# Grouped-query attention, start and sharing of the exponentials: K of group 1 by a transposed load, third chunk by bank, VectorE's exponentials in chunks 3, 9, ... 381

## Chip, cores and metric

The kernel runs on one core of one Trainium2 chip. The metric is the device time of one execution in microseconds (us). All runs are fast ones, at a granted clock of 0.996 or more of the full one.

## The reference

```python
B, Hq, Hkv, Sq, Sk, D = 16, 32, 8, 288, 512, 128      # bf16
k = jnp.repeat(k, rep, axis=1); v = jnp.repeat(v, rep, axis=1)   # rep = 4
scores = jnp.einsum("bhqd,bhkd->bhqk", q, k) * D ** -0.5
out = jnp.einsum("bhqk,bhkd->bhqd", softmax(scores, axis=-1), v)
```

There are 128 groups (16 x 8), each with 1152 queries that share 512 keys and values.

## The kernel before

The scores of a group, transposed, are 4608 columns of 128 partitions, cut into three chunks of 1536 columns (three banks of PSUM, the memory that TensorE writes to; a bank holds 512 of these columns). So there are 384 chunks, 0 to 383. For chunk n TensorE makes the scores (`op_s`), ScalarE takes the exponential, and two chunks later TensorE multiplies P by V (`op_pv`); VectorE divides by the row sums and evicts (`op_rc`, `op_ev`). In every sixth chunk VectorE takes the last 120 columns of the exponential itself, by a polynomial in eight operations.

```python
# TensorE: one chunk of scores, then P times V two chunks behind
for n in range(NS):
    op_s(n)
    if shared(n): op_sy(n)                 # 120 columns into the spare end of a bank of ps_o
    if n == 2: op_kt(1, range(NJ), 1)      # transposes of K, group 1
    if n >= LAG: op_pv(n - LAG)
...
# VectorE, for r in range(NS - 1), n = r + 2
op_rc(r)
if shared(n): op_y(n)
if shared(n - 1): op_yu(n - 1, 1); op_yu(n - 1, 2); op_yp(n - 1)
op_ev(r)
if shared(n): op_yb(n); op_ym(n); op_yu(n, 0)
...
# GpSimd: V of group g from the landing buffer into a padded one
waits = [have("v", g)]
if g >= 2: waits.append(("s_pv", NC * (g - 2) + 2))
emit(eng, waits, lambda: eng.tensor_copy(v_sb[...], vd_sb[...]))
...
# SyncE issues every transfer but two, in a fixed order
first = [q(0), v(0), q(1), k(2..3), v(1..3), q(2), q(3)]       # (shortened)
```

P times V of the first and second chunk of a group also reads part of the next chunk (`place`, `sequence`).

Of the kernel before, what the change touches and what calls it, by code (L numbers as in the profile page):

```python
# [9 lines left out]
BF16 = mybir.dt.bfloat16  # L10
# [121 lines left out]
def bass_standalone__gqa_softmax__near_ridge_kernel(  # L132
# [6 lines left out]
    B, Hq, Sq, D = q.shape  # L139
    _, Hkv, Sk, _ = k.shape  # L140
    P = 128
    R = (Hq // Hkv) * Sq
    NJ = Sk // P
# [8 lines left out]
    NC = COLS // CH  # L152
# [10 lines left out]
    EVERY = 6  # L163
# [3 lines left out]
    UG = 4  # L167
# [2 lines left out]
    NQ = 12  # L170
    NPT = 6
    WARM = 5
    FIRST = 2
    FIRST_SHARED = 6
    AHEAD = 1.08
    NO = 12
    NS = NG * NC
# [5 lines left out]
    k_v = k.rearrange("b g (p j) d -> (b g p) (j d)", j=NJ)  # L183
    kd_v = k.rearrange("b g (p j) d -> p (b g) (j d)", j=NJ)
# [3 lines left out]
    with ExitStack() as es:  # L188
        sem = {}
# [13 lines left out]
            S("us_v%d" % i)  # L203
        for i in range(UG):
            S("s_k%d" % i)
        for name in ["s_v0", "s_v1", "s_s0", "s_y", "s_yb", "s_ym", "s_yu", "s_yp", "s_kd0", "s_kd1", "s_id", "s_kp"]:
            S(name)
        for i in range(NQ):
            S("s_q%d" % i)
# [25 lines left out]
        main = ExitStack()  # L235
        vd_sb = main.enter_context(nc.sbuf_tensor("vd_sb", [P, NSLOT, UG, NJ * D], BF16))
        v_sb = main.enter_context(nc.sbuf_tensor("v_sb", [P, NSLOT, UG * NJ, VP], BF16))
        qt_sb = main.enter_context(nc.sbuf_tensor("qt_sb", [P, NQ, NT, P], BF16))
        kd_sb = main.enter_context(nc.sbuf_tensor("kd_sb", [P, 2, NJ * D], BF16))
        ident = main.enter_context(nc.sbuf_tensor("ident", [P, P], BF16))  # L240
        ones_b = main.enter_context(nc.sbuf_tensor("ones_b", [P, P], BF16))
        kt_sb = main.enter_context(nc.sbuf_tensor("kt_sb", [P, NSLOT, NJ, UG, P], BF16))
# [18 lines left out]
        def need(eng, waits):  # L261

            left = []
            for (s, n) in waits:
                key = (id(eng), s)
                if seen.get(key, 0) < n:
                    seen[key] = n
                    left.append((sem[s], n))
            return left

        def emit(eng, waits, fn):
            waits = need(eng, waits)
            for (s, n) in waits[:-1]:
                eng.wait_ge(s, n)
            ins = fn()
            if waits:
                ins.wait_op(waits[-1][0], waits[-1][1], "sem-ge")
            return ins



        def op_kd(eng, g):
            eng.dma_start(kd_sb[:, g], kd_v[:, g]).then_inc(sem["s_kd%d" % g], 16)

        def op_k(u, g0=0):
            eng = nc.sync
            sl = u % NSLOT
            if u >= NSLOT:
                for (s, n) in need(eng, [("s_s", NC * UG * (u - NSLOT + 1))]):
                    eng.wait_ge(s, n)  # L290
            eng.dma_start_transpose(
                kt_sb[:, sl, :, g0:UG].rearrange("d j g p -> d j (g p)"),
                k_v[(u * UG + g0) * P:(u + 1) * UG * P]
            ).then_inc(sem["us_k%d" % sl if u > 0 else "s_k2"], 16)

        def op_v(u, eng=None, g0=0, g1=UG):
            eng = eng or nc.sync
            sl = u % NSLOT
            if u >= NSLOT:
                for (s, n) in need(eng, [("s_vc", UG * (u - NSLOT + 1))]):  # L300
                    eng.wait_ge(s, n)
            eng.dma_start(
                vd_sb[:, sl, g0:g1], v_v[:, u * UG + g0:u * UG + g1]
            ).then_inc(sem["us_v%d" % sl if u > 0 else "s_v%d" % g0], 16)

        def op_q(g):
            eng = nc.sync
            if g >= NQ:
                for (s, n) in need(eng, [("s_s", NC * (g - NQ + 1))]):
                    eng.wait_ge(s, n)  # L310
            eng.dma_start_transpose(qt_sb[:, g % NQ], q_v[g * P:(g + 1) * P]).then_inc(sem["s_q%d" % (g % NQ)], 16)
# [11 lines left out]
        def have(kind, g):  # L323

            u = g // UG
            if u == 0 and kind == "k":
                return ("s_k%d" % min(g, 2), (2, 1, 16)[min(g, 2)])
            if u == 0:
                return ("s_v%d" % min(g, 1), 16)
            return ("us_%s%d" % (kind, u % NSLOT), 16 * (u // NSLOT + (0 if u % NSLOT == 0 else 1)))  # L330
# [43 lines left out]
        def ready(n, x):  # L374

            if n < FIRST and x < TPC - 1:
                return ("s_eb", n * (TPC - 1) + x + 1)
# [18 lines left out]
            i, c = place(t, j)  # L396
            return pt_sb[:, (g * NC + i) % NPT, c:c + P]

        def op_kt(g, tiles, bank):

            eng = nc.tensor
            dst = ps_o[:, bank].bitcast(BF16)
            for x, j in enumerate(tiles):
                ins = emit(eng, [("s_id", 2), ("s_kd%d" % g, 16)], lambda: eng.transpose(  # L404
                    dst[:, x * P:(x + 1) * P], kd_sb[:, g, j * D:(j + 1) * D], ident[:]))
            ins.then_inc(sem["s_kp"], 1)

        def op_kc(g, tiles, bank, n):
            eng = nc.vector
            src = ps_o[:, bank].bitcast(BF16)[:, 0:len(tiles) * P].rearrange("d (j p) -> d j p", p=P)  # L410
            emit(eng, [("s_kp", n)], lambda: eng.tensor_copy(  # L411
                kt_sb[:, 0, tiles[0]:tiles[-1] + 1, g], src)).then_inc(sem["s_k%d" % g], 1)

        def op_warm(n, w, dst):

# [101 lines left out]


        def shared(n):
            return FIRST_SHARED <= n < NS - NC and (n - FIRST_SHARED) % EVERY == 0  # L520

        def nth(n):
            return (n - FIRST_SHARED) // EVERY + 1
# [100 lines left out]


        first = [lambda: op_q0(0), lambda: op_v(0, None, 0, 1)]
        first += [lambda: op_q(1), lambda: op_k(0, 2), lambda: op_v(0, None, 1, UG), lambda: op_q(2), lambda: op_q(3)]

        sp = []
        for u in range(1, NU):  # L630
# [21 lines left out]
        @block.tensor  # L652
        def _(eng):
            op_warm(WARM, BANK, ps_o[:, 1])
            op_warm(1, P, ps_o[:, 1])
            op_kt(0, range(1), 0)
            op_kt(0, range(1, NJ), 1)
            op_warm(1, P, ps_s[:, 1])
            for n in range(NS):
                op_s(n)  # L660
                if shared(n):
                    op_sy(n)
                if n == 2:
                    op_kt(1, range(NJ), 1)
                if n >= LAG:
                    op_pv(n - LAG)
            op_pv(NS - 2)
            op_pv_last()
            emit(eng, [("s_ev", NS - 2), ("s_bad", 2)], lambda: eng.matmul(  # L669
                ps_o[0:1, NS % 2, 0:ALONE + 1], one_f[:], bad_sb[:, 1, :], start=True, stop=True)  # L670
            ).then_inc(sem["s_bad"], 1)
            choose(eng, "pe")

        @block.scalar
        def _(eng):
            op_kd(eng, 0)
            eng.activation(dum[:], nc.const_aps.tensor(0.0, [P, 1], FP32), ACTF.Exp)
            for (s, n) in need(eng, [("s_k0", 2)]):
                eng.wait_ge(s, n)
            op_kd(eng, 1)  # L680
            for n in range(NS):
                op_exp(n)
            op_ev_act()
            choose(eng, "act")
# [12 lines left out]
        @block.vector  # L697
        def _(eng):
            eng.memset(one_f[:], 1.0)
            op_kc(0, range(1), 0, 1)  # L700
            op_kc(0, range(1, NJ), 1, 2)
            op_kc(1, range(NJ), 1, 3)
            per_b = G * NC
            w0 = NS - 1 - ALONE // TPC
            last = rl_sb[:, NG * NT - ALONE:NG * NT]
            for r in range(NS - 1):
                n = r + LAG
                op_rc(r)
                if shared(n):
                    op_y(n)  # L710
                if shared(n - 1):
                    op_yu(n - 1, 1)
                    op_yu(n - 1, 2)
                    op_yp(n - 1)
                op_ev(r)
                if shared(n):
                    op_yb(n)
                    op_ym(n)
                    op_yu(n, 0)
                if r % per_b == per_b - 1 and r < NS - 1:  # L720
                    op_stat(r // per_b)
                if r == w0:
                    op_stat(B - 1)
                if r == w0 + 1:
                    emit(eng, [("s_stat", B)], lambda: eng.tensor_reduce(
                        ck_sb[:, 0:1], st_sb[:, 0, :], AX.X, ALU.max))
                    eng.tensor_reduce(ck_sb[:, 1:2], st_sb[:, 1, :], AX.X, ALU.min).then_inc(sem["s_stat"], 1)
                if r == w0 + 2:
                    op_over(ck_sb[:, 0:1], ck_sb[:, 1:2], ALONE, ALONE + 1, ("s_stat", B + 1), B + 2)
            op_rc(NS - 1)  # L730
            op_ev_last()
            op_over(last, last, 0, ALONE, ("s_rc", NS), B + 3)
            with nc.allow_low_precision(reason="a count of at most 2048"):
                emit(eng, [("s_bad", 3)], lambda: eng.tensor_reduce(  # L734
                    flag_i[:], ps_o[0:1, NS % 2, 0:ALONE + 1], AX.X, ALU.add)).then_inc(sem["s_flag"], 1)
            choose(eng, "dve")
# [30 lines left out]
```

## Time and profile before

| | before |
|---|---|
| median of three runs | 521.98 us (521.74 to 523.07) |
| span of the profiled run | 519.98 us |
| chunk 7 starts on ScalarE | 14.61 us |
| last chunk starts | 514.87 us |
| from chunk 7 to the last | 500.26 us, 376 chunks, 1.3305 each |
| from the start of the last exponential (third bank, 515.82) to the end | 4.16 us |

The last four rows cut the span into a start, a middle and an end. The prediction shows the lines of the page.

### The profile page before, as it was taken

What the parts mean: (1) busy time and instruction counts of PE and PEld (TensorE: products, weight loads), DVE (VectorE), ACT (ScalarE), POOL (GpSimd) and SP (SyncE); (2) the same over time, 40 slices, a digit from 0 to 9 for tenths busy, and PEclk for the clock granted to TensorE, in tenths of its full rate; (3) what the DMA queues carried; (4) which work ended last, traced back from release to release, by engine and by line L of the source; (5) the groups of instructions that cost most, each with busy time, mean ns of one, the idle gap of its engine ahead of it and who ended that gap; (6) DMA issues with size and microseconds to landing.
All of it is one profiled execution on the core that took longest, in us unless ns stands there. A gap on an engine that the chain in (4) does not pass through costs nothing.

```text
span 520.0 us, 15243 instructions
## 1 busy us (share of the span) xinstructions
PE 510.3 (98%) x6118; PEld 394.6 (76%) x6224; DVE 369.6 (71%) x1315; ACT 513.3 (99%) x393; POOL 79.8 (15%) x135
## 2 busy tenths in 40 slices
PE   8999999999999999999999999999999999999997
PEld 5777777777777777777777777777777777777776
DVE  2767767777777677676776776767767767677776
ACT  7999999999999999999999999999999999999997
POOL 2111111111111111111111111111111111111110
PEclk9999999999999999999999999999999999999999
DMA  9999999999999998999999989999998989998212
GB/s 186 237 218 230 267 194 248 225 213 210 219 233 256 208 245 201 235 248 240 215 241 209 209 225 220 241 185 209 229 240 232 227 194 201 192 234 198 86 69 93
DMA packets 253078, 110.06 MB, mean 212 GB/s; under 512 B 219728, under 2 KB 236752, under 8 KB 253008
## 3 DMA queue, kind: packets, MB, share of 16 engines
q1 hardware_dynamic: 252720, 108.82, 97.7%
q8 instruction: 49, 0.80, 0.7%
q10 hardware_dynamic: 288, 0.26, 0.2%
q14 instruction: 21, 0.17, 0.2%
HBM read 17.04 MB, written 37.75 MB: 105 GB/s over the span
## 4 chain that ended last, share of the span: by engine, by line
ACT 98%; DMA 1%; issue 1%; DVE 0%; PE 0%
ACT pt_sb L516 97%; DMA qt_sb<-in_q_dram 1%; ACT pt_sb L511 1%; PE ps_s L439 0%; DVE o_sb L585 0%; DVE o_sb L595 0%; PE ps_s L479 0%; DVE rl_sb L575 0%; PE ps_o L669 0%; DVE bad_sb L621 0%; DVE flag_i L734 0%; DVE bad_sb L618 0%
## 5 line engine op out<-in xcount | busy, mean ns | idle before, releaser
L516 ACT ACTIVATE pt_sb<-ps_s 128x1536 bf16<-128x1536 f32 (+2 forms) x384 | 508.8, 1441 | 0.0
L479 PE MATMUL ps_o<-v_sb,pt_sb 128*128 128x129 bf16 x4584 | 322.3, 220 | 1.1
L479 PEld LDWEIGHTS ps_o<-v_sb,pt_sb 128*128 128x128 bf16 x4584 | 282.8, 98 | 49.7 <-DVE o_sb L585 14.1
L439 PE MATMUL ps_s<-qt_sb,kt_sb 128*128 128x512 bf16 (+2 forms) x1430 | 290.4, 320 | 5.0 <-DMA qt_sb<-in_q_dram 0.5
L585 DVE TENSOR_TENSOR o_sb<-ps_o,rl_sb 128x384 bf16<-128x384 f32 x382 | 211.9, 555 | 9.3 <-DVE rl_sb L575 0.5
L439 PEld LDWEIGHTS ps_s<-qt_sb,kt_sb 128*128 128x128 bf16 x1536 | 123.9, 98 | 62.3 <-issue 1.1
L575 DVE RECIPROCAL rl_sb<-ps_o 128x3 f32<-128x3 f32 x382 | 68.1, 178 | 125.5 <-PE ps_o L479 124.0
L568 POOL COPY v_sb<-vd_sb 128x512 bf16<-128x512 bf16 x128 | 78.8, 616 | 429.1 <-PE ps_o L479 408.9
L549 DVE SCALAR_TENSOR_TENSOR u_sb<-u_sb,m_sb 128x120 f32<-128x120 f32 x126 | 35.6, 283 | 2.2
L556 DVE SCALAR_TENSOR_TENSOR pt_sb<-u_sb,e_sb 128x120 bf16<-128x120 f32 x63 | 17.8, 283 | 2.2
L549 DVE SCALAR_TENSOR_TENSOR u_sb<-m_sb 128x120 f32<-128x120 f32 x63 | 17.4, 277 | 0.0
L527 DVE TENSOR_SCALAR y_sb<-ps_o 128x120 f32<-128x120 f32 x63 | 15.9, 253 | 0.0
L540 DVE TENSOR_SCALAR m_sb<-t_sb 128x120 int32<-128x120 int32 x63 | 14.1, 223 | 2.2
L540 DVE TENSOR_SCALAR e_sb<-t_sb 128x120 int32<-128x120 int32 x63 | 13.6, 216 | 0.0
L450 PE MATMUL ps_o<-qt_sb,kt_sb 128*128 128x120 bf16 x63 | 13.6, 216 | 0.0
L533 DVE TENSOR_SCALAR t_sb<-y_sb 128x120 int32<-128x120 f32 x63 | 13.4, 213 | 0.0
L450 PEld LDWEIGHTS ps_o<-qt_sb,kt_sb 128*128 128x128 bf16 x63 | 6.2, 98 | 7.4
L511 ACT ACTIVATE pt_sb<-ps_s 128x512 bf16<-128x512 f32 x6 | 3.3, 616 | 2.3 <-PE ps_s L439 2.3
L411 DVE COPY kt_sb<-ps_o 128x128 bf16<-128x128 bf16 (+2 forms) x3 | 1.0, 336 | 6.2 <-PE ps_o L404 6.1
L613 DVE TENSOR_REDUCE st_sb<-rl_sb 128x1 f32<-128x72 f32 (+1 forms) x16 | 3.5, 216 | 0.0
L611 DVE TENSOR_REDUCE st_sb<-rl_sb 128x1 f32<-128x72 f32 (+1 forms) x16 | 3.5, 216 | 0.0
L417 PE MATMUL ps_o<-const-bfloat16-1.0 128*128 128x512 bf16 (+1 forms) x6 | 2.4, 570 | 0.9 <-PEq L752 0.9
(32 smaller groups left out, 12.0 us busy)
## 6 DMA issues: line engine op xcount, KB each, us to landing
out_dram<-o_sb SPq DMA_DIRECT2D x127, 288.0 KB, 3.7
vd_sb<-in_v_dram SPq DMA_DIRECT2D x31, 512.0 KB, 5.5
qt_sb<-in_q_dram SPq DMA_TRANSPOSE x128, 4.9
kt_sb<-in_k_dram SPq DMA_TRANSPOSE x32, 5.1
vd_sb<-in_v_dram SPq DMA_DIRECT2D x1, 384.0 KB, 4.6
out_dram<-o_sb SPq DMA_DIRECT2D x3, 96.0 KB, 1.6
kd_sb<-in_k_dram ACTq DMA_DIRECT2D x2, 128.0 KB, 2.7
vd_sb<-in_v_dram SPq DMA_DIRECT2D x1, 128.0 KB, 3.3
```

Source lines behind the costliest of these rows:

```text
L439: ins = emit(eng, w_x, lambda: eng.matmul(ps_s[:, n % 2, c:c + w], kt_sb[:, sl, j, gi, :], qg[:, t * P:t * P + w], start=True, stop=True))
L450: emit(eng, [("s_ev", n - LAG - 1)], lambda: eng.matmul(ps_o[:, (n - LAG) % 2, BANK - W:BANK], kt_sb[:, (g // UG) % NSLOT, j, g % UG, :], ...
L479: ins = emit(eng, w_x, lambda: eng.matmul(outs(r)[:, t - r % NC * TPC, :], pt(g, t, j), v_sb[:, sl, gi * NJ + j, 0:DV], start=(x == 0), st ...
L516: emit(eng, waits, lambda: eng.activation(d, s, ACTF.Exp, scale=scale)).then_inc(sem["s_e"], 1)
L527: emit(eng, [("s_yb", nth(n) - NB), ("s_pv", n - LAG + 1)], lambda: eng.tensor_scalar(out=y_sb[:, b], in0=ps_o[:, (n - LAG) % 2, BANK - W: ...
L533: emit(eng, [("s_ym", 2 * (nth(n) - NB)), ("s_y", nth(n))], lambda: eng.tensor_scalar(out=t_sb[:, b], in0=y_sb[:, b], scalar1=Y_MUL, scala ...
L540: emit(eng, [("s_yp", nth(n) - NB), ("s_yb", nth(n))], lambda: eng.tensor_scalar(out=dst[:, b], in0=t_sb[:, b], scalar1=mask, scalar2=bits ...
L549: lambda: eng.scalar_tensor_tensor(out=u_sb[:, b, x], in0=src, scalar=QUARTIC[x], in1=m, op0=ALU.add, op1=ALU.mult)
L556: lambda: eng.scalar_tensor_tensor(out=pt_sb[:, n % NPT, CH - W:CH], in0=u_sb[:, b, 2], scalar=QUARTIC[3], in1=e_sb[:, b].bitcast(FP32), o ...
L568: emit(eng, waits, lambda: eng.tensor_copy(v_sb[:, sl, gi * NJ:(gi + 1) * NJ, 0:D], vd_sb[:, sl, gi].rearrange("p (j d) -> p j d", d=D))). ...
L575: emit(eng, [("s_pv", r + 1)], lambda: eng.reciprocal(rl_sb[:, TPC * r:TPC * (r + 1)].unsqueeze(2), outs(r)[:, :, D:DV])).then_inc(sem["s_ ...
L585: emit(eng, waits, lambda: eng.tensor_tensor(out=o_sb[:, g % NO, t0:t0 + TPC, :], in0=outs(r)[:, :, 0:D], in1=rl_sb[:, TPC * r:TPC * (r + ...
```

## The change

Its intent: K of group 1 no longer takes TensorE and VectorE but arrives transposed; the third chunk is exponentiated bank by bank so that what reads it can begin earlier; VectorE helps three chunks sooner and once more at the end.

```diff
-    FIRST = 2
-    FIRST_SHARED = 6
+    FIRST = 3
+    FIRST_SHARED = 3
...
-            return FIRST_SHARED <= n < NS - NC and (n - FIRST_SHARED) % EVERY == 0
+            return FIRST_SHARED <= n < NS - 2 and (n - FIRST_SHARED) % EVERY == 0
...
-        first += [op_q(1), op_k(0, 2), op_v(0, None, 1, UG), op_q(2), op_q(3)]              # "lambda:" left out
+        first += [op_q(1), op_k(0, 1, 2), op_v(0, None, 1, UG), op_k(0, 2), op_q(2), op_q(3)]
...
-                if n == 2:
-                    op_kt(1, range(NJ), 1)
...
-            for (s, n) in need(eng, [("s_k0", 2)]):
-                eng.wait_ge(s, n)
-            op_kd(eng, 1)
...
-            op_kc(1, range(NJ), 1, 3)
```

(The rest of the diff fits the helpers to one direct load of K.)

More of the change, by code (lines that the diff above doesn't have):

```diff
@@ L205, in bass_standalone__gqa_softmax__near_ridge_kernel @@
             S("s_k%d" % i)
-        for name in ["s_v0", "s_v1", "s_s0", "s_y", "s_yb", "s_ym", "s_yu", "s_yp", "s_kd0", "s_kd1", "s_id", "s_kp"]:
+        for name in ["s_v0", "s_v1", "s_s0", "s_y", "s_yb", "s_ym", "s_yu", "s_yp", "s_kd0", "s_id", "s_kp"]:
             S(name)
@@ L238, in bass_standalone__gqa_softmax__near_ridge_kernel @@
         qt_sb = main.enter_context(nc.sbuf_tensor("qt_sb", [P, NQ, NT, P], BF16))
-        kd_sb = main.enter_context(nc.sbuf_tensor("kd_sb", [P, 2, NJ * D], BF16))
+        kd_sb = main.enter_context(nc.sbuf_tensor("kd_sb", [P, NJ * D], BF16))
         ident = main.enter_context(nc.sbuf_tensor("ident", [P, P], BF16))
@@ L278, in emit, with op_kd, op_k @@
             return ins
-        def op_kd(eng, g):
-            eng.dma_start(kd_sb[:, g], kd_v[:, g]).then_inc(sem["s_kd%d" % g], 16)
-        def op_k(u, g0=0):
+        def op_kd(eng):
+            eng.dma_start(kd_sb[:], kd_v[:, 0]).then_inc(sem["s_kd0"], 16)
+        def op_k(u, g0=0, g1=UG):
             eng = nc.sync
@@ L291, in op_k @@
             eng.dma_start_transpose(
-                kt_sb[:, sl, :, g0:UG].rearrange("d j g p -> d j (g p)"),
-                k_v[(u * UG + g0) * P:(u + 1) * UG * P]
-            ).then_inc(sem["us_k%d" % sl if u > 0 else "s_k2"], 16)
+                kt_sb[:, sl, :, g0:g1].rearrange("d j g p -> d j (g p)"),
+                k_v[(u * UG + g0) * P:(u * UG + g1) * P]
+            ).then_inc(sem["us_k%d" % sl if u > 0 else "s_k%d" % g0], 16)
         def op_v(u, eng=None, g0=0, g1=UG):
@@ L326, in have @@
             if u == 0 and kind == "k":
-                return ("s_k%d" % min(g, 2), (2, 1, 16)[min(g, 2)])
+                return ("s_k%d" % min(g, 2), (2, 16, 16)[min(g, 2)])
             if u == 0:
@@ L397, in pt, with op_kt @@
             return pt_sb[:, (g * NC + i) % NPT, c:c + P]
-        def op_kt(g, tiles, bank):
+        def op_kt(tiles, bank):
             eng = nc.tensor
@@ L403, in op_kt, with op_kc @@
             for x, j in enumerate(tiles):
-                ins = emit(eng, [("s_id", 2), ("s_kd%d" % g, 16)], lambda: eng.transpose(
-                    dst[:, x * P:(x + 1) * P], kd_sb[:, g, j * D:(j + 1) * D], ident[:]))
+                ins = emit(eng, [("s_id", 2), ("s_kd0", 16)], lambda: eng.transpose(
+                    dst[:, x * P:(x + 1) * P], kd_sb[:, j * D:(j + 1) * D], ident[:]))
             ins.then_inc(sem["s_kp"], 1)
-        def op_kc(g, tiles, bank, n):
+        def op_kc(tiles, bank, n):
             eng = nc.vector
@@ L411, in op_kc @@
             emit(eng, [("s_kp", n)], lambda: eng.tensor_copy(
-                kt_sb[:, 0, tiles[0]:tiles[-1] + 1, g], src)).then_inc(sem["s_k%d" % g], 1)
+                kt_sb[:, 0, tiles[0]:tiles[-1] + 1, 0], src)).then_inc(sem["s_k0"], 1)
         def op_warm(n, w, dst):
@@ L626, in bass_standalone__gqa_softmax__near_ridge_kernel @@
         first = [lambda: op_q0(0), lambda: op_v(0, None, 0, 1)]
-        first += [lambda: op_q(1), lambda: op_k(0, 2), lambda: op_v(0, None, 1, UG), lambda: op_q(2), lambda: op_q(3)]
+        first += [lambda: op_q(1), lambda: op_k(0, 1, 2), lambda: op_v(0, None, 1, UG), lambda: op_k(0, 2), lambda: op_q(2), lambda: op_q(3)]
         sp = []
@@ L655, in _ @@
             op_warm(1, P, ps_o[:, 1])
-            op_kt(0, range(1), 0)
-            op_kt(0, range(1, NJ), 1)
+            op_kt(range(1), 0)
+            op_kt(range(1, NJ), 1)
             op_warm(1, P, ps_s[:, 1])
@@ L675, in _ @@
         def _(eng):
-            op_kd(eng, 0)
+            op_kd(eng)
             eng.activation(dum[:], nc.const_aps.tensor(0.0, [P, 1], FP32), ACTF.Exp)
-            for (s, n) in need(eng, [("s_k0", 2)]):
-                eng.wait_ge(s, n)
-            op_kd(eng, 1)
             for n in range(NS):
@@ L699, in _ @@
             eng.memset(one_f[:], 1.0)
-            op_kc(0, range(1), 0, 1)
-            op_kc(0, range(1, NJ), 1, 2)
-            op_kc(1, range(NJ), 1, 3)
+            op_kc(range(1), 0, 1)
+            op_kc(range(1, NJ), 1, 2)
             per_b = G * NC
```

## The prediction

> **What bounds the kernel now.** I read the page from the top: shares by engine, the chain of waits that ended last, then the groups by form, and last the timeline of the first 26 us and of the last 8, and single starts of ScalarE in narrow windows.
>
> ```profile
> PE 510.3 (98%) x6118; PEld 394.6 (76%) x6224; DVE 369.6 (71%) x1315; ACT 513.3 (99%) x393; POOL 79.8 (15%) x135
> ...
> ACT 98%; DMA 1%; issue 1%; DVE 0%; PE 0%
> ```
>
> Two engines look full, ScalarE (99%) and TensorE (98%), and the chain names ScalarE alone. A pipelined engine can look full while it is paced by another, so I ask the timeline who really waits. First the start of ScalarE, then its steady pace with the score matmuls (L439) that feed it:
>
> ```profile
> 5.05 1.09 ACT L511 ACTIVATE pt_sb<-ps_s 128x512 bf16<-128x512 f32 x2 [2.33 <-PE ps_s L439]
> 6.50 1.10 ACT L511 ACTIVATE pt_sb<-ps_s 128x512 bf16<-128x512 f32 x2
> 7.93 1.51 ACT L516 ACTIVATE pt_sb<-ps_s 128x1536 bf16<-128x1536 f32 x1
> 9.26 1.52 ACT L516 ACTIVATE pt_sb<-ps_s 128x1536 bf16<-128x1536 f32 x1
> 10.59 1.53 ACT L516 ACTIVATE pt_sb<-ps_s 128x1536 bf16<-128x1536 f32 x1
> 11.93 1.54 ACT L516 ACTIVATE pt_sb<-ps_s 128x1536 bf16<-128x1536 f32 x1
> 13.26 1.45 ACT L516 ACTIVATE pt_sb<-ps_s 128x1416 bf16<-128x1416 f32 x1
> 14.61 1.45 ACT L516 ACTIVATE pt_sb<-ps_s 128x1536 bf16<-128x1536 f32 x1
> ...
> 13.04 0.88 PE L479 MATMUL ps_o<-v_sb,pt_sb 128*128 128x129 bf16 x12
> 13.76 0.81 PE L439 MATMUL ps_s<-qt_sb,kt_sb 128*128 128x512 bf16 x2
> 14.41 0.84 PE L479 MATMUL ps_o<-v_sb,pt_sb 128*128 128x129 bf16 x12
> 15.09 0.82 PE L439 MATMUL ps_s<-qt_sb,kt_sb 128*128 128x512 bf16 x6
> ```
>
> Columns: start, length, engine, line, instruction. Number the chunks 0 to 383. Chunks 0 and 1 are exponentiated by bank; six banks from 5.05 to 7.93 are 0.48 us each. Chunk 2 starts at 7.93 and chunk 6 at 13.26: (13.26 - 7.93)/4 = 1.333 us per full chunk. There ScalarE is back to back. The slope between the two sizes is (1.333 - 0.48)/1024 = 0.83 ns a column, so a chunk short of the 120 columns that VectorE takes should cost 1.333 - 0.10 = 1.233 us.
>
> It does not. Chunk 6 is such a chunk, and chunk 7 starts 1.35 us after it, not 1.23. The scores of chunk 7 start at 13.76 and end at 14.57; the exponential follows at 14.61. From there TensorE sets the pace: 0.65 us of scores and 0.68 us of P times V alternate with no gap, 1.33 us per chunk. ScalarE starts chunk 12 at 21.28 and chunk 18 at 29.26, 7.98 us for six chunks with one shared one, where its own work would be 5 x 1.333 + 1.233 = 7.90. From chunk 6 (13.26) to the last (514.87) the mean is 501.61/377 = 1.3305 us. So: the first seven chunks belong to ScalarE, and the rest to TensorE, with ScalarE 0.08 us in six chunks below it. That the chain says ScalarE comes from instructions that overlap their predecessor and so show no idle time.
>
> **What the Trainium skill says.** "ScalarE: Activation LUTs", What ACT_TABLE_LOAD costs, gives 0.833 ns an element plus 186 ns with immediate scale and bias, less some 93 ns where instructions follow closely. The trace agrees in slope (0.83) and length (616 ns for 512 columns); its overlap is larger, 616 - 480 = 136 ns, and I use the trace. "TensorE: Matmul & The Clock Gate", Back-to-back issue gap, gives columns/2.4 + 2.5 ns for warm matmuls. An estimate from that page for six chunks: 72 of 129 columns at 56.3 ns, 16 of 512 at 215.8, 8 of 128 at 55.8, = 7.95 us; the trace has 7.98, so TensorE has 0.03 us of slack in six chunks. By the same formula splitting 512 columns into 392 and 120 costs one more 2.5 ns. "DMA: Bandwidth & Descriptors", Issuing engines are not separate DMA queues, says that the queues share the 16 engines; so a load that ScalarE no longer issues also frees time for the transposed ones.
>
> **Part 1, K of group 1.** Removed: ScalarE's second load of K, four transposes on TensorE and one copy on VectorE.
>
> ```profile
> 7.30 0.23 PEld L404 LDWEIGHTS ps_o<-ident,kd_sb 128*128 128x128 bf16 x4 [0.16 <-DMA kd_sb<-in_k_dram]
> 7.31 0.40 PE L404 MATMUL ps_o<-ident,kd_sb 128*128 128x128 bf16 x4
> 7.49 0.72 PEld L479 LDWEIGHTS ps_o<-v_sb,pt_sb 128*128 128x128 bf16 x12
> 7.54 0.84 PE L479 MATMUL ps_o<-v_sb,pt_sb 128*128 128x129 bf16 x12
> 8.28 0.34 PEld L439 LDWEIGHTS ps_s<-qt_sb,kt_sb 128*128 128x128 bf16 x3
> 8.31 0.81 PE L439 MATMUL ps_s<-qt_sb,kt_sb 128*128 128x512 bf16 x3
> ```
>
> The transposes hold TensorE from 7.31 to 7.54, 0.23 us, with 0.16 of waiting for the load ahead. That is in ScalarE's stretch: the scores of chunk 3 end at 9.12 and are used at 9.26. So up to 0.23 us is freed on an engine that is not yet the limit. Added: one transposed load of 128 KB. In the DMA view the transposed load issued at 4.21 (groups 2 and 3, 256 KB) landed 4.1 us later, at 8.3, and the second queries, issued at 2.86, landed 3.8 later, at 6.66. One group alone should take half of the 1.64 us between these: an estimate of 7.5. Chunk 3's scores would start at 8.31 - 0.23 = 8.1 at the earliest and must start by about 8.5. So it is in time, with 0.6 to 1 us to spare. Groups 2 and 3 and the third queries then move back by perhaps 0.4 us; the latter landed at 6.22 + 5.1 = 11.3 and are used at 12.39. Still in time. Gain on the path: 0.
>
> **Part 2, chunk 2 by bank.** Cost on ScalarE: 3 x 0.48 = 1.44 instead of 1.333, so +0.10 us. Gain: the P times V of chunk 1 reads part of chunk 2 and need no longer wait for all of it (at 8.96 it took 0.94 instead of 0.84 us, 0.10 of waiting), and the scores of chunk 4 can begin bank by bank.
>
> **Part 3, VectorE's share.** 64 shared chunks (3, 9, ... 381) instead of 63 (6, ... 378). ScalarE has 0.10 us less in chunk 3, which repays part 2: chunk 4 again starts at 5.05 + 9 x 0.48 + 1.233 = 10.6 (10.59 before), chunk 6 at 13.26, chunk 7 at 13.26 + 1.333 = 14.59 (14.61 before, set by TensorE). TensorE cannot come earlier either: P times V of chunks 3 and 4 reads chunks 4 and 5, whose exponentials end at 10.59 + 1.53 = 12.12 and 11.93 + 1.54 = 13.47 as before; with about 0.06 us of signal and the last four matmuls, 0.23 us, the scores of chunk 7 start at 13.76, as they do now. After that TensorE's work per chunk is unchanged. At the end, the shared chunk 381 shortens ScalarE by 0.10 us where TensorE is the limit, so 0; VectorE gets eight small operations just before its last evictions:
>
> ```profile
> 515.74 0.56 DVE L585 TENSOR_TENSOR o_sb<-ps_o,rl_sb 128x384 bf16<-128x384 f32 x1
> ...
> 516.47 0.18 DVE L575 RECIPROCAL rl_sb<-ps_s 128x3 f32<-128x3 f32 x1 [0.17 <-PE ps_s L479]
> ```
>
> After a shared chunk in the middle VectorE is back in step three evictions later with 0.37 us of idle time (at 25.93), so here it should just be back by 516.47: 0 to +0.05.
>
> Sum: start -0.02, middle 0, end 0 to +0.05: nothing. 521.98 becomes 521.9, within the spread of the three runs.
>
> **Rivals.** (a) TensorE keeps the time that it is freed: the removed transposes (0.23) and the shorter wait (0.10) come off, 521.65. For it: from chunk 7 on TensorE is the limit, so every earlier start counts to the end. Against: chunks 4 to 6 are tied to exponentials that start no earlier. (b) ScalarE is the limit throughout, as the chain says; then one more shared chunk takes 0.10 off and the split puts 0.10 on: 521.98. Against it: 7.98 and not 7.90 for six chunks. (c) K of group 1, or the third queries behind it, land late: chunk 3 or 6 waits, and all of it reaches the end because TensorE never recovers: +0.3 to +1, up to 523. Against it: the margins above; for it: the DMA engines are busy nine tenths of the time in most slices. (d) VectorE's result for chunk 3 is late for P times V of chunk 3: it comes about 2.5 us after P times V of chunk 1 ends (14.06 to 16.44 for chunk 6), so near 12.1, when that product waits for chunk 4 anyway: at most +0.1.
>
> **Range and chances.** The largest honest gain is 0.3 us and the likely loss below 1; the runs of before spread over 1.3 us, one of three being 1.1 above the median. So 521.2 to 522.8. A change of 2% would be 10 us, thirty times any term here: faster 0.005, within 0.985, slower 0.01.
>
> **What would show it.** Chunk 3's exponential at about 9.37, chunks 4 to 6 at 10.6, 11.93 and 13.26 again, chunk 7 at 14.6, six chunks at 7.98, the last at about 514.85. If chunk 7 comes at 14.3 to 14.5 and the lead is kept, (a) is right; if six chunks fall to 7.90, my reading of TensorE as the limit is wrong; a wait for a load at chunk 3 or 6 is (c).

## The result, and the profile after

The changed kernel took 522.32 us (522.31 to 522.36, four runs), the kernel before 521.86 in the same rounds (521.69 to 523.07). The ratio is 1.0004 (interval 0.9987 to 1.0021): the same. Ratios are the mean time of one kernel's runs over that of the other's of the same rounds, so they are not quite the ratio of the medians quoted; with one of the runs before at 523.07, the means differ by 0.21 us where the medians differ by 0.46. The time lies in the stated range; the centre, 521.9, was 0.4 too low, and the experiments ask where that came from.

The page after, shares by engine and the chain of waits:

```profile
PE 510.5 (98%) x6115; PEld 394.6 (76%) x6221; DVE 370.6 (71%) x1322; ACT 513.4 (99%) x395; POOL 79.5 (15%) x135
...
PE 97%; issue 1%; DVE 1%; DMA 1%
```

The shares are the same as before, but the chain now names TensorE and not ScalarE. I take it that two limits so close together let a chain tip either way. What did change is seen in the timeline. First ScalarE around chunk 13, before:

```profile
21.28 1.39 ACT L516 ACTIVATE pt_sb<-ps_s 128x1416 bf16<-128x1416 f32 x1
22.59 1.45 ACT L516 ACTIVATE pt_sb<-ps_s 128x1536 bf16<-128x1536 f32 x1
```

and after, with what the other engines did just ahead of it:

```profile
19.63 0.89 DVE L549 SCALAR_TENSOR_TENSOR u_sb<-u_sb,m_sb 128x120 f32<-128x120 f32 x2
19.70 0.68 POOL L568 COPY v_sb<-vd_sb 128x512 bf16<-128x512 bf16 x1 [5.02 <-DMA vd_sb<-in_v_dram]
...
21.35 0.68 PEld L479 LDWEIGHTS ps_o<-v_sb,pt_sb 128*128 128x128 bf16 x12 [0.51 <-DVE o_sb L585]
...
21.39 1.45 ACT L516 ACTIVATE pt_sb<-ps_s 128x1536 bf16<-128x1536 f32 x1
22.89 1.45 ACT L516 ACTIVATE pt_sb<-ps_s 128x1536 bf16<-128x1536 f32 x1
```

Chunk 12 starts 0.11 us later than before (21.39 against 21.28), chunk 13 already 0.30 later, and the last chunk is still 0.30 later (515.17 against 514.87). So the loss in the middle is one event of 0.19 us. (The table below counts the middle from chunk 7, which was 0.07 late: +0.23.) Two steps of VectorE's polynomial for chunk 9 took 0.89 us together instead of 0.60 (one of them 572 ns instead of 283), at the moment at which GpSimd copied a V that had just landed; VectorE's next eviction came late, and TensorE waited 0.51 us for it instead of about 0.22 (the lines of e10 below show the undisturbed 0.60 and 0.22).

Then the end: SyncE's issues of the last three stores, before and after.

```profile
516.40 0.33 SPq L343 DMA_DIRECT2D out_dram<-o_sb  x1
517.27 0.33 SPq L343 DMA_DIRECT2D out_dram<-o_sb  x1
517.83 0.33 SPq L343 DMA_DIRECT2D out_dram<-o_sb  x1
```

```profile
516.91 0.33 SPq L343 DMA_DIRECT2D out_dram<-o_sb  x1
517.54 0.33 SPq L343 DMA_DIRECT2D out_dram<-o_sb  x1
518.39 0.33 SPq L343 DMA_DIRECT2D out_dram<-o_sb  x1
```

Before, the last two are 0.55 apart (0.56 by the rounded lines) and the last follows its data (evicted by 517.79) at once. After, they are 0.85 apart and the data (ready at 518.06) wait 0.33 us. From the start of the last exponential to the end it is 4.50 us instead of 4.16: the last store is issued 0.26 us later after it, and takes 1.81 instead of 1.73 us to land. SyncE's last branch follows this landing by 0.02 us in every profile, so it is this store that the end waits for. So the span's +0.64 us is: start +0.11 (up to chunk 12), middle +0.19, end +0.34.

### The profile page after: what moved, and what is told of

It is laid out like the page before. It is cut to its first block, busy times and chain, and to the rows that moved or that the text cites. A ratio compares the mean times of both kernels' runs of the same rounds, so it can differ in the third digit from the quotient of the medians.

```text
span 520.6 us, 15248 instructions
## 1 busy us (share of the span) xinstructions
PE 510.5 (98%) x6115; PEld 394.6 (76%) x6221; DVE 370.6 (71%) x1322; ACT 513.4 (99%) x395; POOL 79.5 (15%) x135
## 4 chain that ended last, share of the span: by engine, by line
PE 97%; issue 1%; DVE 1%; DMA 1%
PE ps_o L479 50%; PE ps_s L439 46%; DMA qt_sb<-in_q_dram 1%; PE ps_o L450 1%; DVE o_sb L585 0%; DVE u_sb L549 0%; DVE rl_sb L575 0%; DVE o_sb L595 0%; DVE pt_sb L556 0%; DVE t_sb L533 0%; PE ps_o L667 0%; DVE m_sb L540 0%; DVE bad_sb L621 0%; DVE flag_i L728 0%; DVE y_sb L527 0%
## 5 line engine op out<-in xcount | busy, mean ns | idle before, releaser
L511 ACT ACTIVATE pt_sb<-ps_s 128x512 bf16<-128x512 f32 x8 | 4.4, 620 | 2.4 <-PE ps_s L439 2.4
```

## The experiments

The first theory: the middle is lost to VectorE and GpSimd disturbing each other in the odd groups, which the new sharing has moved to; the end is lost to VectorE's late last evictions. The rivals are in the expectations. All runs gave correct results, and every verdict at 2% was "same".

| kernel | chunk 3 | chunk 7 | chunk 7 to last | last exp. to end | gap of last stores | all runs, sorted (us) |
|---|---|---|---|---|---|---|
| before | 9.26 | 14.61 | 500.26 | 4.16 | 0.55 | 521.74 521.98 523.07 |
| after | 9.40 | 14.68 | 500.49 | 4.50 | 0.85 | 522.31 522.32 522.32 522.36 |
| e1 without 381 | 10.29 | 15.68 | 500.43 | 4.66 | 0.85 | 522.33 to 523.82 (6) |
| e2 one copy held | 9.23 | 14.81 | 500.50 | 4.51 | 0.85 | 522.35 to 523.71 (6) |
| e3 part 1 alone | 9.22 | 14.57 | 500.27 | 4.71 | 0.85 | 522.07 522.10 522.12 522.20 522.32 |
| e4 every twelfth | 10.73 | 16.05 | 502.03 | 4.05 | 0.55 | 523.70 to 524.78 (5) |
| e5 SyncE plus one | 9.71 | 15.03 | 500.26 | 4.80 | 0.85 | 522.22 to 522.97 (5) |
| e6 V by ScalarE | 12.14 | 17.46 | 500.27 | 4.14 | 0.55 | 522.52 to 525.77 (6) |
| e7 same, sharing from 3 | 10.01 | 15.40 | 500.53 | 4.08 | 0.55 | 522.66 to 525.67 (6) |
| e8 96 columns | 9.27 | 14.59 | 500.26 | 4.15 | 0.55 | 521.63 521.92 522.52 522.80 523.04 |
| e9 waits on GpSimd | 10.58 | 15.97 | 500.55 | 4.36 | 0.55 | 522.17 522.28 523.04 523.24 523.53 |
| e10 same, copies held | 9.27 | 14.55 | 500.29 | 4.36 | 0.56 | 521.74 521.85 521.98 522.13 522.21 |
| e11 part 1, waits on GpSimd | 9.26 | 14.60 | 500.27 | 4.40 | 0.56 | 521.88 521.92 522.10 522.21 522.69 |
| e12 part 3 alone | 9.68 | 15.34 | 500.80 | 4.08 | 0.55 | 522.23 522.25 522.92 523.05 523.14 |

The columns from the traces are one profiled execution each. They separate what the run times mix: the start (chunks 3 and 7) jumps by over a microsecond between executions, the middle is steady to a few hundredths (500.26 to 500.29) except in e4 and where the odd groups share with the copies free, and the end falls into groups by SyncE's stream, as e5 shows. The runs of before over all rounds were 521.5 to 523.3.

**e1: no shared chunk at the end.**

```diff
-            return FIRST_SHARED <= n < NS - 2 and ...
+            return FIRST_SHARED <= n < NS - NC and ...
```

> The changed kernel without the last shared chunk (381): VectorE shares 3, 9, ... 375. Theory 1 (the late exponential delays VectorE's eviction of chunk 380, so the store of group 126 is issued at 516.15 instead of about 515.0 and the last store at 518.39, 0.33 us after its data): the stores follow their data again, the last exponential stays at 515.17, and the time falls by 0.25 to 0.3 us, from 522.3 to about 522.0. Rival (the flag chain sets the end, and it is 0.27 later only because the last exponential is 0.30 later): the time stays at 522.3.

Measured 523.03 (ratio 1.0011). The end took 4.66 us, not less than the 4.50 after, and the last stores stayed 0.85 apart. VectorE's late evictions are not the cause of the longer end: that theory falls. Nor is the rival quite right, since the last store is late by itself. This execution also shows the jump at the start:

```profile
8.37 1.28 PE L479 MATMUL ps_o<-v_sb,pt_sb 128*128 128x129 bf16 x12
...
10.29 2.83 ACT L516 ACTIVATE pt_sb<-ps_s 128x1416 bf16<-128x1416 f32 x2 [0.57 <-PE ps_s L439]
```

Twelve products took 1.28 us instead of 0.84: TensorE was still at its slow rate, in which a weight load takes 151 ns instead of 98. The last such load was at 5.7 us in the profile of before, at 6.6 after, at 9.1 here, between 3.4 and 9.6 over all profiles. Where it is past 9 (e1, e4, e6, e9) chunk 3 comes at 10.3 or later; in e6 a late load adds to it.

**e2: one copy of V held back.**

```diff
-                waits.append(("s_pv", NC * (g - 2) + 2))
+                waits.append(("s_pv", NC * (g - 2) + (4 if g == UG else 2)))
```

> The changed kernel, with GpSimd's copy of V of group 4 held back by two products, so that it no longer runs beside VectorE's polynomial of chunk 9 (19.63 to 20.5). Theory 1 (the two engines disturb each other: one polynomial step took 572 ns instead of 283): no step over 300 ns, chunk 13 starts at about 22.65 instead of 22.89, the last exponential at 514.95, the time falls by 0.2 to 0.25 us to about 522.1. Rival (the product of chunk 9 or 10 is held up by VectorE's own chain, the copy only coincides): chunk 13 stays at 22.9, the time at 522.3.

Measured 522.52 (1.0008): no gain. Chunk 9 was indeed undisturbed, but the next load of V landed in chunk 21 (and two steps of chunk 3 took 529 and 524 ns beside the copies of groups 1 and 2):

```profile
34.99 0.62 POOL L568 COPY v_sb<-vd_sb 128x512 bf16<-128x512 bf16 x1 [4.23 <-DMA vd_sb<-in_v_dram]
35.08 0.60 DVE L540 TENSOR_SCALAR m_sb<-t_sb 128x120 int32<-128x120 int32 x1
...
37.47 0.68 PEld L479 LDWEIGHTS ps_o<-v_sb,pt_sb 128*128 128x128 bf16 x12 [0.59 <-DVE o_sb L585]
```

The operation took 597 ns instead of 223, and ScalarE's pitch, the time from one chunk's start to the next, was 1.58 us once (at 39.01). The miss supports the collision as such; it had only moved. In this execution the third queries, issued at 7.41, landed at 12.56, and TensorE waited 0.20 us for them before chunk 6, though the start of this kernel is that of the changed one: the second half of rival (c).

**e3: part 1 alone.** The changed kernel with `FIRST = 2`, `FIRST_SHARED = 6` and `NS - NC`.

> Part 1 alone: K of group 1 by a transposed load; chunks 0 and 1 by bank and sharing in 6, 12, ... 378 as before. As predicted: chunk 3's scores start at 8.1 instead of 8.31, chunk 3's exponential still at 9.26, chunk 7's still at 14.6: 521.9, a ratio of 1.000. Rival a (TensorE keeps what it is freed of): chunk 7 at 14.4, 521.65 or less. Rival c (a load is late): chunk 3 or 6 waits, over 522.2.

Measured 522.12 (0.9995). Start and middle are as predicted: chunk 3 at 9.22, chunk 7 at 14.57 (9.56 us after the first exponential, as before), 500.27 us from there on. Rival (a), that TensorE keeps what it is freed of, is refuted. But the end takes 4.71 us, with the sharing where it was before. Part 1 alone brings the longer end.

**e4: every twelfth chunk shared.** `EVERY = 12` in the kernel before.

> The kernel before, with VectorE sharing every twelfth chunk instead of every sixth (32 shared chunks instead of 63). If TensorE sets the pace from chunk 7 on, as predicted, ScalarE needs 11 x 1.333 + 1.233 = 15.90 us for twelve chunks and TensorE 15.96: the time stays within 0.2 us of before. If ScalarE sets the pace, as the chain of waits says, 31 chunks cost 0.10 us more each: +3.1 us, 525.

Measured 523.97 (1.0029), from chunk 7 to the last 502.03 us: +1.77, neither 0 nor 3.1. The lines of the steady stretch say why (ScalarE, start and length):

```profile
149.57 1.48 ACT L516 ACTIVATE pt_sb<-ps_s 128x1536 bf16<-128x1536 f32 x1
150.90 1.49 ACT L516 ACTIVATE pt_sb<-ps_s 128x1536 bf16<-128x1536 f32 x1
152.23 1.51 ACT L516 ACTIVATE pt_sb<-ps_s 128x1536 bf16<-128x1536 f32 x1
153.56 1.52 ACT L516 ACTIVATE pt_sb<-ps_s 128x1536 bf16<-128x1536 f32 x1
154.89 1.53 ACT L516 ACTIVATE pt_sb<-ps_s 128x1536 bf16<-128x1536 f32 x1
```

The starts are 1.33 us apart, but each is 13 ns longer than the one before. The ends are 1.343 apart. I read this so: a start is when the instruction is taken in behind its predecessor, and the ends show the engine's own pace. So ScalarE needs 11 x 1.343 + 1.244 = 16.02 us for twelve chunks, over TensorE's 15.97, and the trace repeats every 16.022 us. For six chunks it needs 5 x 1.343 + 1.244 = 7.96, under the measured 7.98.

**e5: one more instruction for SyncE in the kernel before.**

```diff
+            eng.wait_ge(sem["s_id"], 2)
+            eng.wait_ge(sem["s_v0"], 16)
+            eng.wait_ge(sem["s_qp0"], 16)
             for (_, fn) in sp:
```

(Two of these three waits fit one instruction and the third is carried by the next transfer.)

> The kernel before, with one more instruction in SyncE's stream (a wait that has long been satisfied, after the first loads). All kernels with part 1 so far have one more instruction there than before, and their last store follows the one ahead of it by 0.85 us instead of 0.56, with data that are ready; the end comes 0.5 us later. If the place of SyncE's instructions in the stream does that, this kernel shows the gap of 0.85 as well and takes 0.3 to 0.5 us more than the fast runs of before (522.1 instead of 521.7). Rival (the transposed load itself, or what it moves in the queues, does it): the gap stays 0.56 and the time 521.7.

Measured 522.59 (1.0005). The last stores of this kernel:

```profile
516.83 0.33 SPq L343 DMA_DIRECT2D out_dram<-o_sb  x1
517.70 0.33 SPq L343 DMA_DIRECT2D out_dram<-o_sb  x1
518.54 0.33 SPq L343 DMA_DIRECT2D out_dram<-o_sb  x1
```

The gap of 0.85 is there without any transposed load, and the end takes 4.80 us. Between a wait that is over at 518.20 and this issue SyncE shows nothing for 0.34 us (0.05 before); after it, its load of the flag takes 0.73 us instead of 0.47 (0.71 to 0.73 in every kernel with the wide gap). The end grows by more than the gap because the last store also lands later, 2.07 us after its issue instead of 1.73 (1.81 to 2.07 in the kernels with the wide gap, 1.61 to 1.73 in the others). Sorted by the instructions that the traces list for SyncE: 339 in before, e4, e6, e7, e8 and e12, with an end of 4.05 to 4.16; 340 in after, e1, e2, e3 and e5, with 4.50 to 4.80. So it is the place of SyncE's instructions in its stream, one further than before.

That a fetch of instructions falls into the last issues is what I suppose. The DMA packets in the traces fit that, without showing it: in the five kernels with 340, an 8 KB packet of the instruction queue q14 starts while SyncE loads the flag (519.03 to 519.45 us in after), and in the other nine the last such packet starts only after that load (519.14 in before); but it comes after the issue that was late.

In this execution the kernel before also lost 0.45 us at chunk 3 (9.71) to a second load of K that landed late: TensorE waited 0.77 us for it. Part 1 removes that wait.

**e6: V of groups 1 to 3 by ScalarE's queue, part 1 alone.**

```diff
-  ..., op_k(0, 1, 2), op_v(0, None, 1, UG), op_k(0, 2), ...
+  ..., op_k(0, 1, 2), op_k(0, 2), ...
+            for (s, n) in need(eng, [("s_k0", 2)]): eng.wait_ge(s, n)     # on ScalarE
+            op_v(0, eng, 1, UG)
```

> Part 1 alone, with V of groups 1 to 3 loaded by ScalarE where it loaded K of group 1 before, so that SyncE has as many instructions as in the kernel before. If SyncE's stream is what makes part 1 slower at the end: the last two stores are 0.56 apart again and the time is that of the fast runs of before, 521.6 to 521.8, some 0.4 less than part 1 alone (522.1). Rival (the transposed load does it): 522.1 again. The third queries, no longer behind V, land by 11.5.

Measured 523.21 (1.0025). The end is 4.14 us and the gap 0.55, so the first half holds, but the start is ruined:

```profile
11.30 0.81 PE L439 MATMUL ps_s<-qt_sb,kt_sb 128*128 128x512 bf16 x3 [1.45 <-DMA kt_sb<-in_k_dram]
...
12.14 1.45 ACT L516 ACTIVATE pt_sb<-ps_s 128x1536 bf16<-128x1536 f32 x1 [2.05 <-PE ps_s L439]
```

Beside 384 KB of V the second queries landed 6.0 us after their issue instead of 3.8, and K of group 1 after 7.0 instead of 3.1 in the changed kernel. This is rival (c), made by hand. Not all of it is the load: TensorE was also at its slow rate until 9.5 us in this execution. In e7, with the same loads but at full rate from 4.9 us on, TensorE waited 1.49 us for K and chunk 3 came 0.74 us late. That the order in the change, K of group 1 ahead of V, keeps the transposed load in time is argued from this; with that order K landed at 7.3 to 7.9 us in all profiles.

**e7: the same with sharing from 3 to 375.** `FIRST_SHARED = 3` on top of e6.

> As the last one, but VectorE shares 3, 9, ... 375 instead of 6, ... 378. ScalarE then leads by 0.10 us from chunk 4 on, but TensorE's products of chunks 3 and 4 need chunks 4 and 5: if the start gives nothing and GpSimd's copies disturb VectorE in the odd groups, as supposed, the time is 0.2 to 0.3 above the last one (521.9 to 522.1), with one or two steps of VectorE over 500 ns in the first 40 us. Rival (the earlier sharing is good, only the other parts hurt): 521.5 or less.

Measured 522.96 (1.0026). The start is spoilt as in e6 (chunk 3 at 10.01), so the time tells nothing of the sharing; the middle does: 500.53 instead of 500.27, with one operation of 618 ns at 19.7. As expected, the earlier sharing gives the middle nothing and costs 0.26.

**e8: 96 instead of 120 columns for VectorE.** `W = 96` in the kernel before.

> The kernel before with 96 instead of 120 columns of a shared chunk on VectorE. With every twelfth chunk shared the ends of the exponentials were 1.343 us apart, so ScalarE needs 5 x 1.343 + 1.244 = 7.959 us in six chunks where the kernel takes 7.983. With 96 columns it needs 0.02 us more, 7.979, still just under: if TensorE sets the pace, the time stays within 0.2 us of before. If ScalarE does: 63 x 24 x 0.83 ns = +1.26 us.

Measured 522.52 (1.0007), the runs from 521.63 as before, and exactly 500.26 us from chunk 7 to the last, though ScalarE does more. TensorE sets the pace of the middle in the kernel before, by about 0.02 us in six chunks.

**e9: SyncE's waits for earlier stores on GpSimd, all three parts.**

```diff
-        sp.append((NS - NC + LAG + 2.5, op_stored))
+            for (s, n) in need(eng, stored()): eng.wait_ge(s, n)      # GpSimd, after its last copy
```

> The changed kernel, all three parts, with the four waits for the earlier stores moved from SyncE to GpSimd, so that SyncE's stream is shorter than in the kernel before. In all ten profiles so far the time from the start of the last exponential to the end of the span is 4.05 to 4.16 us where SyncE has its old number of instructions and 4.50 to 4.79 where it has one more. If the place in the stream is the cause: 4.0 to 4.2 here, with the last two stores 0.56 apart, and 521.8 to 522.0 instead of 522.3. Rival (it is the three parts of the change, VectorE's late evictions among them): 4.5 and 522.3.

Measured 523.04 (1.0001); this execution had a slow start (last slow weight load at 9.6). The stores are 0.55 apart again and the load of the flag takes 0.47, but the end takes 4.36, not 4.1: now SyncE's step from the last branch to the end takes 0.75 us instead of 0.41. The traces list 335 instructions for SyncE here and in e10 and e11. Half of the loss had moved a few instructions on, which again speaks for the place in the stream.

**e10: as e9, the copies of the first group of each load held.** `4 if g % UG == 0 else 2` in the wait of e2.

> As e9, and GpSimd's copy of the first group of each load of V is held until the product of the shared chunk beside it has been made (all such groups, not the first alone as in e2). If the collisions are what the changed kernel still loses: no step of VectorE's polynomial over 350 ns, no pitch of ScalarE over 1.45 us after chunk 7, and 0.2 us less than e9: 521.6 to 521.8, the fast runs of before. Rival: as e9.

Measured 521.98, between 521.74 and 522.21; before, in the same job, 521.86 to 522.99 over nine runs; ratio 0.9989 (0.9975 to 1.0002). No pitch over 1.45 us after chunk 7, and 500.29 us from there on, the value of the kernels without sharing in the odd groups. Chunk 9, with its copy held until after it:

```profile
19.49 0.60 DVE L549 SCALAR_TENSOR_TENSOR u_sb<-u_sb,m_sb 128x120 f32<-128x120 f32 x2
...
20.62 0.61 POOL L568 COPY v_sb<-vd_sb 128x512 bf16<-128x512 bf16 x1 [6.08 <-PE ps_o L479]
...
20.93 0.78 PEld L479 LDWEIGHTS ps_o<-v_sb,pt_sb 128*128 128x128 bf16 x12 [0.22 <-DVE o_sb L585]
```

The collisions are the loss of the middle. One step did take 671 ns, at 10.2 in chunk 3, beside the copies of groups 1 and 2, which I had not held; it cost nothing that the middle shows. The median, 521.98, is above the 521.6 to 521.8 expected, since the end is 4.36.

**e11: part 1 alone, waits on GpSimd.** e3 with the edit of e9.

> Part 1 alone (e3) with the waits for the stores on GpSimd. Should have neither the collisions of the odd groups nor the longer end, and no wait for the second load of K at chunk 3: 521.5 to 521.7, the best of all here if the start is warm in time, e3 less 0.4. Rival (part 1 is itself slower): 522.1.

Measured 522.10 (0.9992), 521.88 at best: not the 521.5 to 521.7 expected, since the end is 4.40 here too. Start and middle are those of before.

**e12: part 3 alone.** `FIRST_SHARED = 3` and `NS - 2` in the kernel before.

> Part 3 alone: the kernel before, with VectorE sharing 3, 9, ... 381. SyncE's stream is that of before, so the end should take 4.05 to 4.2 us although VectorE's last evictions are late. In the first 40 us at least one step of VectorE over 500 ns beside a copy of GpSimd, in chunk 9 or 21, and ScalarE's pitch over 1.45 us two to four chunks later: 0.2 to 0.3 us more than the fast runs of before, 521.9 to 522.0. Rival (collisions are rare or harmless): 521.7. Rival (VectorE's late evictions at the end cost): an end of 4.4 or more.

Measured 522.92 (1.0001), 522.23 at best. The middle:

```profile
20.03 0.65 POOL L568 COPY v_sb<-vd_sb 128x512 bf16<-128x512 bf16 x1 [4.70 <-PE ps_o L479]
...
20.24 0.89 DVE L549 SCALAR_TENSOR_TENSOR u_sb<-u_sb,m_sb 128x120 f32<-128x120 f32 x2
...
21.97 0.68 PEld L479 LDWEIGHTS ps_o<-v_sb,pt_sb 128*128 128x128 bf16 x12 [0.51 <-DVE o_sb L585]
```

Here both chunk 9 and chunk 21 were hit (572 and 640 ns), and the middle takes 500.80: +0.54, about 0.27 for each. A third step, 521 ns in chunk 3 beside the copies of groups 1 and 2, fell into the start: TensorE waited 0.60 us for VectorE's eviction at 13.80, and chunk 7 came 1.60 us after chunk 6 instead of 1.39 in the profile after. The end takes 4.08 although VectorE evicts late: SyncE's stream is that of before.

No version beats both kernels clearly. e10 is the best of the changed ones and cannot be told from before. Part 2 alone was not run.

## Why the prediction was right or wrong

**What bounds the kernel: right in the name, wrong in the margin.** TensorE does set the middle (e8: 500.26 again). The failed step is "ScalarE 0.08 us in six chunks below it". It rests on a pace of 1.333 us read from starts; the ends in the prediction's own lines (7.93 + 1.51, 9.26 + 1.52, ...) are 1.343 apart, and the margin is 0.02. e4 fell for that reason: ScalarE needs 16.02 us for twelve chunks, not 15.90.

**Part 1: right.** K was in time (landed 3.1 us after its issue at 4.25, at 7.32; 7.5 was estimated), and freeing TensorE in ScalarE's stretch brought nothing: chunk 7 at 14.57 in e3. Rival (a) is refuted. Rival (c) was real. For K it did not happen in the change; e6 and e7 show its size, 1.45 and 1.49 us of waiting. For the third queries the margin was misjudged: they landed 0.65 us later than before (12.02 against 11.37), not 0.4, in time for chunk 6 in the profile after but 0.20 us late in e2.

**Part 2: its mechanism was right.** P times V of chunk 1 took 0.84 us again (0.94 before), and the third chunk took three banks from 7.97 to 9.40. But the predicted cost, +0.10, again comes from starts: by ends three banks take 1.470 us and the whole chunk 1.343, so +0.13. Its part in the time was not isolated.

**Part 3, the start: slightly missized.** Chunk 7 was to come at 14.59 and came at 14.68. As the prediction says, the scores of chunk 7 wait for P times V of chunk 4, and that for chunk 5's exponential, which ended at 13.54 instead of 13.47. Of these 0.074 us, 0.047 is a first exponential that came later in this execution, and 0.027 is that part 2 cost 0.13 where the shared chunk 3 gave back only 0.10. Such sizes lie far within the jump of the start between executions.

**Part 3, the middle: the failed term.** "After that TensorE's work per chunk is unchanged" holds for TensorE, and yet 0.19 us went. The prediction asked whether VectorE's result for chunk 3 would be late (rival d, at most +0.1; e12 shows some 0.2 where a copy ran beside them) but not what else runs beside the operations once they lie in the odd groups. The page "SBUF — State Buffer", section "Who interferes with whom", says that VectorE and GpSimd share one pair of ports, and that a VectorE operation with two inputs in SBUF, or one in a two-port mode, blocks against a GpSimd operation that reads SBUF. The trace agrees: the scalar-tensor-tensor steps went from 283 to 572 ns and one tensor-scalar from 223 to 597, all beside a copy of GpSimd. In all profiles twelve steps took over 300 ns; a copy had begun before each of them, and each ended 73 to 134 ns after that copy's end, as if it had waited for it. The step that reads its scores from PSUM ran beside a copy 63 times in the kernel before and took 251 to 254 ns each time. (That the tensor-scalar steps run in a two-port mode is not shown here, only that they were stretched.) The copies that follow a load come when the load lands, at about 19.5 and 35; in the kernel before that is between two shared chunks, in the changed one it can be within chunks 9 and 21 (in the profile after, the second came at 34.38, early enough to spare chunk 21). e10, e12 and e7 show it.

**Part 3, the end: right for its own reason, wrong in sum.** VectorE's late evictions cost nothing (e12: 4.08 us at the end; e1 without chunk 381: no gain). But the sum "end 0 to +0.05" missed 0.34, which comes with one more instruction in SyncE's stream (e5: +0.64 in the kernel before). I found no view of the profile before that shows it; why the place matters stays open.

**The range** was set by the spread of the runs, and that was right. That the time lies in it is owed to its width: the sum, "nothing", missed +0.19 in the middle and +0.34 at the end. The source of that spread is the start: the profiles tie it to when TensorE reaches its full rate and when the first loads land. For the slow runs of before themselves this is argued only, since none of them was the profiled one.

## What to carry to other kernels

Read an engine's own pace from the ends of its instructions, not from the starts: overlapped starts hide a queue that grows. Before you move work of VectorE, look at what GpSimd does at the new times, above all copies that are released by a landing transfer. At this size of effect cut the span into start, middle and end and compare these; whole run times mix a start that jumps by a microsecond and more with an end that depends on where the last instructions lie.

## What the Trainium skill lacked or had wrong

- "ScalarE: Activation LUTs", What ACT_TABLE_LOAD costs: back-to-back instructions are said to overlap by about 93 ns. Here ends are 0.490 us apart for 512 columns and 1.343 for 1536, that is 0.833 ns a column plus 63 ns; with the page's 186 ns an overlap of about 123.
- "Runtime: NRT & Kernel Launch", Instruction fetch mechanics, calls the cost of crossing a block of instructions mostly hidden. No page that I found has the place of an instruction in SyncE's stream as a cost at the end of a kernel: one more instruction took the time from the last exponential to the end from 4.05 to 4.16 us up to 4.50 to 4.80. That this is such a crossing is not shown.
- "TensorE: Matmul & The Clock Gate", Part 1, says that the change to full rate comes around 4 us into sustained activity and varies by about 0.5 us from run to run. TensorE's activity is not unbroken here (it waited 0.42 to 0.59 us for queries at about 4.5 us), and over the profiles the last slow weight load lies between 3.4 and 9.6 us; where it came last (e1, e4, e9) chunk 3 was 1.0 to 1.5 us later than before.
- "TensorE: Matmul & The Clock Gate", Back-to-back issue gap, keeps the formula that the prediction used for a single matmul and gives about 81 ns (128 columns) and 131 ns (512) for a stream with weight loads. Here the stream follows the formula: starts are 57 ns apart after a product of 129 columns and 216 ns after one of 512.
